# Where expert weights wait for room: four xt tiles, one tile of turned g, and w_out's product in halves

## The chip, the cores and the metric

The kernel runs on one core of a Trainium2 chip. The metric is the device time of one execution in microseconds. Times come from three runs, and the rows from one execution recorded by the hardware profiler. The engines are TensorE (PE; PEld is its weight load), VectorE (DVE), ScalarE (ACT), GpSimd (POOL) and SyncE (SP), which issues every load and store here.

## What is computed

Three parts follow one another. The tokens are 4 x 576 = 2304, and the width is 512.

```python
q, k = rotate(q), rotate(k)                         # 4 x 8 heads x 576 x 64
attn = softmax(q @ k.T / 8, axis=-1); x = attn @ v  # x: 2304 x 512
h = x @ w_in                                        # w_in: 512 x 2048
g = maximum(h, 0) + alpha * minimum(h, 0)
x = g @ w_out                                       # w_out: 2048 x 512
logits = x @ phi                                    # phi: 512 x 32 (8 experts x 4 slots)
d = softmax(logits, axis=0)                         # over the tokens
slot_input = (d.T @ x).reshape(8, 4, 512)
for e in range(8):
    slot_out[e] = maximum(slot_input[e] @ w1[e], 0) @ w2[e]   # 512 x 1024, 1024 x 512
c = softmax(logits, axis=1)                         # over the slots
out = c @ slot_out.reshape(32, 512)
```

The expert weights w1 and w2 are 32 MB in fp32. They are the largest input by far. The weights w_in and w_out come as 8-byte floats.

## The kernel before

**The order of the work.** The kernel is written as operations of a planner (`Plan`, lines 49 to 165). Each operation has an engine, a cost, a due time, the operations that it depends on, and the room that it `takes` or `uses` in a class of buffers. The planner plays them through in time. On each engine it takes, among the operations that are ready and whose room is free, the one with the lowest due time. The order found in this way is fixed in the program, one stream for each engine; SP's stream is all loads and stores in order. A load that must wait for its buffer holds up all that stands behind it on SP.

**Attention and feed-forward.** Attention runs until about 510 us. Its results are `xt` tiles, 8 blocks of 256 tokens, and a ninth block (`blks[8]`, tile `xtail`) of the tails of all four batches. `chunk_events` (line 712) handles a block in 16 chunks f of 128 of the 2048 hidden columns: `ph` = x times w_in (L734, three fp16 products), `rl` on ACT (L742), `g` on DVE (L747). Every second chunk is turned: four transposes `pt` (L753), copied by ACT into a tile `gt` (L758). Two `gt` tiles of 8 KB per partition hold a block, one from f=1, one from f=9. Every fourth chunk adds to the logits `lg` (L764), which are `g` times `wph`, the product of w_out and phi.

w_out itself is never applied to a token. `dispatch_events` (line 777) takes the logits: `lp` (DVE, L802), `lgt` (PE, L806), maximum, exponentials `edt` (ACT, L840), transposes `pd` (L845), `dn` (DVE, L852). Then `pu` (L858) multiplies the weights of the slots by the turned `gt`, and `sacc` (DVE, L867) sums over the blocks. `sacc` (32 slots x 2048) is multiplied by w_out only once, at the end: `pa` (transposes, L1078), `at` (DVE, L1084, four pieces c), `px` (16 matmuls in a loop over g, then c, L1090), which reads eight tiles `wo` of w_out, `xs` (L1095), `pst` (L1100), `phs` (L1107).

**Experts.** `expert_in(j)` for two halves j of w1's output: `ph` (32 matmuls, L1126, steps kc of eight), relu into `xtail`'s space (L1143 ACT, L1145 DVE), transposes `pth` (L1150), and copies that end in `hz` (L1160), a zeroed tile with a slot's values on a diagonal. `expert_out(ch)` for two halves of the output columns: `po` (64 matmuls each, L1180), then `mov` (L1209), the combine `pf` (L1292), `ob` (L1297 DVE, L1299 ACT) and the stores (L1305, L1311). The combine's softmax (`pe`, L1267, `est`, L1271) lies beside the experts.

**Room for weights.** Expert weights `xw` (L1033) are loaded by SP in the order of their use: w1, then w2, in halves of 512 KB (4 KB per partition), or 1 MB where a buffer has room for both halves. `cls_of` (line 1004) says where each goes:

- "x": 26 buffers of 4 KB (`x=2*NB`, NB=13), where attention's buffers were. They also take 16 raw loads of w_out (`late_w`, line 969) and the eight `wo` tiles, so they come round a second time.
- "xt": the four `xt` tiles when their blocks are done. Two take weights; two take the zeroed `hz` (`zero`, line 1064, a memset on POOL).
- "w" and "raw": seven buffers of 8 KB (NW=7): the four quarters of w_in, and three that the `gt` tiles go round in. Loads of class "raw" wait in the plan until the last block's last turn.

The program's addresses say what follows whom. Of the 8 KB buffers, two are held by the last block's `gt` until its `pu` are done. Two of the loads of 1 MB wait for that.

In the trace an fp32 matmul has two records, so eight `pu` show as x16.

## Time and profile before

| | |
|---|---|
| three runs | 671.57 us median (671.46 to 677.29) |
| profiled execution, span from the first to the last instruction | 671.6 us |
| profiled execution, its own time with what lies around the span | 673.49 us |
| busy: PE, DVE, ACT, POOL | 611.0 (91%), 456.0 (68%), 360.5 (54%), 287.8 us (43%) |
| chain that ended last, by engine | PE 71%, DVE 9%, DMA 7%, POOL 6%, ACT 4%, SP's queue 2% |
| mean granted clock of TensorE | 0.963 of 2.4 GHz |
| DMA over the span | 146.57 MB, mean 218 GB/s |

The page gives one execution. A share is an average over stages with different limits; the stage that a change touches is read by itself, in tables of busy time by stretch and in the chain of waits, which follows the work that ended last back from the last instruction. A granted clock of 1.00 is 2.4 GHz and 0.50 is 1.2 GHz; a stretch in between has seen both.

### The profile page before, as it was taken

The numbers are of one execution on the slowest core, as the hardware profiler recorded it, in microseconds if no ns is written. First come the engines' busy times: TensorE is split into PE (matmuls) and PEld (weight loads), VectorE is DVE, ScalarE is ACT, GpSimd is POOL, SyncE is SP. The second block draws the span as 40 slices with busy tenths as digits, with TensorE's granted clock in tenths as the row PEclk, the third lists the DMA queues.
The fourth block names the chain that finished last, engine by engine and source line by source line (L and its number), as shares of the span: only waits on it lengthen the run. The fifth ranks groups of instructions, "written<-read, shape, count | busy, mean of one in ns | idle before, by whom it ended". The sixth has DMA issues, their size and how long they took to land.

```text
span 671.6 us, 13543 instructions
## 1 busy us (share of the span) xinstructions
PE 611.0 (91%) x5072; PEld 433.9 (65%) x5072; DVE 456.0 (68%) x989; ACT 360.5 (54%) x868; POOL 287.8 (43%) x283
## 2 busy tenths in 40 slices
PE   2879968979999999999999999999999999988984
PEld 1545444545888678686767868777776868753452
DVE  4776798787878777877576787677736884334332
ACT  2536545645687686775757676684643434330211
POOL 0698999374647656466353655522320000000000
PEclk9898988978999999999999999999999999999997
DMA  8954274530489796877867784777576984447998
GB/s 294 372 182 136 78 238 135 167 112 15 148 253 271 252 242 191 241 196 214 245 182 216 211 250 134 220 193 205 158 189 252 410 333 150 149 149 301 356 395 295
DMA packets 72672, 146.57 MB, mean 218 GB/s; under 512 B 8352, under 2 KB 37536, under 8 KB 72608
## 3 DMA queue, kind: packets, MB, share of 16 engines
q1 hardware_dynamic: 72608, 145.72, 68.3%
q8 instruction: 40, 0.66, 0.4%
q14 instruction: 24, 0.20, 0.1%
HBM read 108.73 MB, written 29.88 MB: 206 GB/s over the span
## 4 chain that ended last, share of the span: by engine, by line
PE 71%; DVE 9%; DMA 7%; POOL 6%; ACT 4%; SPq 2%; issue 2%; DVEq 0%; ACTq 0%; POOLq 0%
PE ph L734 26%; PE pv L573 13%; PE st L431 7%; PE pt L753 4%; DMA xw<-in_moe_w_dram 4%; PE lg L764 3%; PE pu L858 3%; POOL e L473 3%; PE st L418 3%; PE pt L494 2%; PE pc L537 1%; PE ph L1126 1%; PE rest L267 1%; DMA vt<-in_v_dram 1%; PE st L427 1%
## 5 line engine op out<-in xcount | busy, mean ns | idle before, releaser
L473 POOL TENSOR_SCALAR e<-e,mm 128x576 f32<-128x576 f32 x144 | 122.8, 865 | 152.7 <-DVE mm L449 112.1
L734 PE MATMUL ph<-xt,w 128*128 128x256 f16 x1536 | 184.5, 273 | 1.1 <-DVE g L747 0.4
L734 PEld LDWEIGHTS <-w 128*128 128x128 f16 x1728 | 163.9, 98 | 33.4 <-issue 11.8
L436 DVE TENSOR_REDUCE mm<-st 128x1 f32<-128x576 f32 x144 | 106.2, 742 | 27.6 <-PE st L431 21.4
L441 ACT ACTIVATE e<-st,mm 128x576 f32<-128x576 f32 x144 | 106.3, 739 | 29.4 <-DVE mm L436 26.5
L747 DVE SCALAR_TENSOR_TENSOR g<-rl,oma,ph 128x256 f32<-128x256 f32 x144 | 68.2, 474 | 59.6 <-ACT rl L742 59.0
L321 POOL TENSOR_TENSOR xn<-xn,tabs 128x576 f32<-128x576 f32 x60 | 90.3, 1519 | 30.6 <-DMA xn<-in_q_dram 14.9
L742 ACT ACTIVATE rl<-ph 128x256 f32<-128x256 f32 x144 | 55.0, 382 | 88.0 <-PE ph L734 87.6
L431 PE MATMUL st<-ks,qs 128*128 128x288 f32 x384 | 71.7, 314 | 0.3 <-ACT e L441 0.3
L481 DVE STREAM_TRANSPOSE tb<-e 128x512 f32<-128x512 f32 x96 | 66.6, 700 | 3.7 <-POOL e L473 3.0
L573 PE MATMUL pv<-ET,vt 128*64 128x256 f32 x512 | 63.9, 393 | 2.6 <-DVE qs L346 1.2
L418 PE MATMUL st<-ks 64*128 64x288 f32 (+1 forms) x168 | 46.9, 504 | 16.3 <-DVE ks L329 11.5
L431 PEld LDWEIGHTS st<-ks,qs 128*128 128x128 f32 x384 | 54.7, 191 | 4.7 <-issue 2.4
L758 ACT ACTIVATE gt<-pt 128x512 f32<-128x512 f32 x72 | 43.0, 597 | 15.7 <-PE pt L753 14.2
L573 PEld LDWEIGHTS pv<-ET,vt 128*64 128x64 f32 x512 | 35.6, 139 | 24.3 <-issue 6.1
L418 PEld LDWEIGHTS st<-ks 64*128 64x128 f32 (+1 forms) x168 | 26.7, 216 | 30.2 <-DVE ks L329 11.5
L753 PE MATMUL pt<-idf,g 128*128 128x128 f32 x288 | 43.8, 275 | 0.6 <-DVE g L747 0.4
L753 PEld LDWEIGHTS pt<-idf,g 128*128 128x128 f32 x288 | 33.3, 141 | 4.2 <-issue 1.2
L324 POOL TENSOR_TENSOR xn<-xn 128x576 f32<-128x576 f32 x24 | 35.6, 1482 | 0.9
L494 PE MATMUL pt<-idf,e 128*128 128x128 f32 x192 | 33.0, 306 | 3.3 <-POOL e L473 3.1
L494 PEld LDWEIGHTS pt<-idf,e 128*128 128x128 f32 x192 | 25.1, 159 | 15.1 <-POOL e L473 8.1
L349 ACT ACTIVATE ks<-xn 64x576 fp32r<-64x576 f32 x48 | 32.6, 680 | 0.7
(161 smaller groups left out, 840.2 us busy)
## 6 DMA issues: line engine op xcount, KB each, us to landing
sc<-tb SPq DMA_DIRECT2D x48, 512.0 KB, 4.3
ET<-sc SPq DMA_DIRECT2D x96, 256.0 KB, 5.4
xw<-in_moe_w_dram SPq DMA_DIRECT2D x42, 512.0 KB, 10.1
xn<-in_k_dram SPq DMA_DIRECT2D x16, 576.0 KB, 5.0
xn<-in_q_dram SPq DMA_DIRECT2D x16, 576.0 KB, 4.4
wraw<-in_moe_w_in_dram SPq DMA_DIRECT2D x8, 1024.0 KB, 7.1
wraw<-in_w_out_t_dram SPq DMA_DIRECT2D x8, 1024.0 KB, 5.4
wor<-in_moe_w_out_dram SPq DMA_DIRECT2D x16, 512.0 KB, 10.2
```

Of the source, the lines that this page charges most:

```text
L321: eng.tensor_tensor(e["x"][:, w], e["x"][:, w], tabs[:, (0 if z == "q" else 2) + w], ALU.mult)
L418: nc.tensor.matmul(st[to, j, at:at + w], x, k[rows, z:z + w], start=True, stop=True)
L431: nc.tensor.matmul(st[:, j, 0:288], r["q"][:, 768 * h + 128 * s:768 * h + 128 * s + 128].bitcast(F32R), r["k"][:, a, h, ks].bitcast(F32R), ...
L436: nc.vector.tensor_reduce(c["mm"][:, h:h + 1], c["st", h][:, :, 0:288], axis=AX.XY, op=ALU.max, negate=True)
L441: nc.scalar.activation(c["e"][:, h].rearrange("p (a n) -> p a n", a=2), c["st", h][:, :, 0:288], AF.Exp, bias=c["mm"][:, h:h + 1], accum_o ...
L473: nc.gpsimd.tensor_scalar(c["e"][:, h], c["e"][:, h], c["mm"][:, 6 + h:7 + h], 1.0, ALU.mult, ALU.mult)
L481: nc.vector.transpose(out=c["tb"][:, :, h].rearrange("p (q m) j -> p q m j", q=4), in_=c["e"][:, h, 64 * h:64 * h + 512].rearrange("p (m q ...
L494: nc.tensor.transpose(c["pt", h][:, i], c["e"][:, h, 64 * h + 128 * i:64 * h + 128 * i + 128], idf)
L573: nc.tensor.matmul(pv[r], v[k, 4 * h + i if i < 4 else 8], x, start=(i == 0), stop=(i == 4))
L734: nc.tensor.matmul(ph, wi[j][:, wp, kc, 128 * fo:128 * fo + 128], xt[:, xp, kc, :], start=(n == 0), stop=(n == 3 * KC - 1),)
L747: nc.vector.scalar_tensor_tensor(blk["g", j][:, fo, :], c["r"], oma[:, f:f + 1], c["ph"], ALU.mult, ALU.add)
L753: nc.tensor.transpose(c["pt"][:, t, i, :], blk["g", j][:, fo - 1 + i, 128 * t:128 * t + 128], idf)
```

## The change

1. The x pool gets a 27th buffer of 4 KB per partition.
2. `hz`, both halves, moves from two `xt` tiles into one 8 KB buffer of class "raw". Its memsets wait for the last block's `sacc` (`run["gathered"]`). The four loads of class "xt", which shared two tiles in two rounds, have a tile each. The class "w" takes six loads of 1 MB in place of seven.
3. Raw loads wait in the plan for the last block's turn of f=9 (`turn9`) in place of its last turn.
4. The last block's turns with f above 8, and their copies, get a due time 100 later.
5. `late_w` takes the room of `wo` together with that of its raw load.
6. `at` and `xs` lie in the two halves of `xtail`'s space and need no buffers of their own.
7. `px` is cut into two halves: `turned_a(z)` and `mult_s(z)`, z = 0, 1, with c in the outer loop and g in the inner one. The four `wo` tiles 2g+0 are free after the first half.

```diff
--- before.py
+++ after.py
@@ -208,7 +208,7 @@
 
     plan = Plan(dict(
         xn=3, Q=2, K=2, vt=5, e=3, tb=2, sc=4, ET=2, ec=3, ett=1, tabs=1, st=2, mm=8, pm=3, lg=1, xt=4, w=4, raw=NW - 4,
-        wf=1, rl=2, g=2, wt=1, lp=1, lt=1, edt=1, dn=1, dg=1, x=2 * NB, h1=2, mov=1, tmp=1))
+        wf=1, rl=2, g=2, wt=1, lp=1, lt=1, edt=1, dn=1, dg=1, x=2 * NB + 1, h1=2, mov=1, tmp=1))
     op = plan.op
     PE, ACT, DVE, POOL, DMA = "PE", "ACT", "DVE", "POOL", "DMA"
     FIRST = -10000.0
@@ -779,9 +779,12 @@
         blk["g_op"].append(o)
         if fo % 2:
             s_pt = Slot("pm")
-            o = op(PE, 430, due + 2.5, turn, blk["g_op"][-2:] + [raw_done, blk.get("turn")], takes=[s_pt] + ([s_gt] if f % 8 == 1 else []), uses=[s_pt, s_g, s_gt])
+            late = 100 if blk is blks[8] and f > 8 else 0
+            o = op(PE, 430, due + 2.5 + late, turn, blk["g_op"][-2:] + [raw_done, blk.get("turn")], takes=[s_pt] + ([s_gt] if f % 8 == 1 else []), uses=[s_pt, s_g, s_gt])
             blk["turn"] = o
-            blk["gt_op"].append(op(ACT, 600, d, turned, [o], uses=[s_pt, s_gt]))
+            if f == 9:
+                blk["turn9"] = o
+            blk["gt_op"].append(op(ACT, 600, due + 100 if late else d, turned, [o], uses=[s_pt, s_gt]))
         if fo == 3:
             blk["lg_op"] = op(PE, 430, due + 2.5, logit, blk["g_op"][-4:] + [blk["lg_op"]] + [wph_ops[f - i] for i in range(4)],
                               takes=[] if j else [blk["s_lg"]], uses=[blk["s_lg"], s_g])
@@ -951,7 +954,7 @@
 
     def close_att():
         att_stack.close()
-        xp["p"] = ctx.enter_context(tc.tile_pool(name="xp", bufs=2 * NB))
+        xp["p"] = ctx.enter_context(tc.tile_pool(name="xp", bufs=2 * NB + 1))
         fin["z"] = ctx.enter_context(tc.tile_pool(name="hzp", bufs=1))
         fin["sT"] = phs
         fin["ht"] = wph[:].rearrange("p f s -> p (f s)")[:, 0:256].rearrange("p (k c g i) -> p k c g i", k=4, c=4, g=4)
@@ -990,8 +993,8 @@
                 nc.vector.scalar_tensor_tensor(x, hi, -0x40000000, x, ALU.bitwise_and, ALU.bitwise_or)
 
         d = 990 + 0.1 * f
-        o = order_ops["wo"] = op(DMA, 1456, d, load, [att_done, order_ops.get("wo")], takes=[s_raw], uses=[s_raw])
-        o = op(DVE, 450, d, lambda: conv(0), [o, wo_op.get(j)], takes=[] if z else [s_wo[j]], uses=u)
+        o = order_ops["wo"] = op(DMA, 1456, d, load, [att_done, order_ops.get("wo")], takes=[s_raw] if z else [s_raw, s_wo[j]], uses=u)
+        o = op(DVE, 450, d, lambda: conv(0), [o, wo_op.get(j)], uses=u)
         o = op(DVE, 750, d, lambda: conv(1), [o], uses=u)
         wo_op[j] = op(DVE, 700, d, lambda: conv(2), [o], uses=u)
 
@@ -1002,7 +1005,7 @@
     NT = 2
 
     def cls_of(i):
-        return "xt" if NX <= i < NX + NT else "w" if NX + NT <= i < NX + NT + NW else "x"
+        return "xt" if NX <= i < NX + NT else "w" if NX + NT <= i < NX + NT + NW - 1 else "x"
 
     for base in range(0, len(order), 4):
         for half in range(2):
@@ -1036,7 +1039,7 @@
                 for cut in range(n):
                     due = 1000 + base + 2 * half + 0.2 * (i - base) + (2 * cut if n > 1 else 0)
                     ops.append(op(DMA, 1456 * len(parts) / n, due, lambda cut=cut, load=load: load(cut),
-                                  [att_done, blks[8]["turn"] if slot.cls == "raw" else None] + ops[-1:],
+                                  [att_done, blks[8]["turn9"] if slot.cls == "raw" else None] + ops[-1:],
                                   takes=[] if cut else [slot], uses=[slot]))
                 for part in parts:
                     s_ew[key, part], ew_op[key, part] = slot, ops
@@ -1059,14 +1062,16 @@
 
     fin_open = op(None, 0, 0, open_fin, [o for o in plan.ops if any(s.cls in moe_classes for s in o.uses)])
 
-    hz_zero, s_hz = [], [Slot("xt"), Slot("xt")]
+    hz_zero, s_hz = [], [Slot("raw")] * 2
 
     def zero(j):
-        fin["hz", j] = xtp.tile([128, 8, 4, 4, 8], F32, tag="xt", name="hz")
+        if j == 0:
+            fin["hzs"] = wgt.tile([128, 2, 8, 4, 4, 8], F32, tag="w", name="hz")
+        fin["hz", j] = fin["hzs"][:, j]
         nc.gpsimd.memset(fin["hz", j], 0.0)
 
     for j in range(2):
-        hz_zero.append(op(POOL, 900, 1000, lambda j=j: zero(j), [att_done], takes=[s_hz[j]], uses=[s_hz[j]]))
+        hz_zero.append(op(POOL, 900, 1000, lambda j=j: zero(j), [run["gathered"]] + hz_zero, takes=[] if j else [s_hz[j]], uses=[s_hz[j]]))
     sr = cst.tile([128, 2], F32, name="sr")
     D2 = 2000.0
 
@@ -1077,21 +1082,22 @@
         for c in range(4):
             nc.tensor.transpose(fin["pa"][:, c].rearrange("p g s -> p (g s)"), run["acc"][:, 128 * c:128 * c + 128], idf)
 
-    def turned_a():
-        fin["at"] = fin["p"].tile([128, 4, 4, NS], F32, name="at")
-        for c in range(4):
+    def turned_a(z):
+        if z == 0:
+            fin["at"], fin["xs"] = fin["h1"][:, 1].rearrange("p (c g s) -> p c g s", c=4, g=4), fin["h1"][:, 0]
+        for c in (2 * z, 2 * z + 1):
             iv = inv_w[:].rearrange("p (g h) -> p h g", h=2)[:, c // 2]
             nc.vector.tensor_tensor(fin["at"][:, c], fin["pa"][:, c], iv.unsqueeze(2).to_broadcast([128, 4, NS]), ALU.mult)
 
-    def mult_s():
-        fin["px"] = ps_m.tile([128, DM], F32, tag="pm", name="px")
-        for g in range(4):
-            for c in range(4):
-                nc.tensor.matmul(fin["px"][32 * c:32 * c + 32, :], fin["at"][:, c, g, :], wo[2 * g + c // 2][:, c % 2, :],
-                                 start=(g == 0), stop=(g == 3), tile_position=(0, 32 * c))
+    def mult_s(z):
+        if z == 0:
+            fin["px"] = ps_m.tile([128, DM], F32, tag="pm", name="px")
+        for c in (2 * z, 2 * z + 1):
+            for g in range(4):
+                nc.tensor.matmul(fin["px"][32 * g:32 * g + 32, :], fin["at"][:, c, g, :], wo[2 * g + z][:, c % 2, :],
+                                 start=(c == 0), stop=(c == 3), tile_position=(0, 32 * g))
 
     def kept_s():
-        fin["xs"] = fin["p"].tile([128, DM], F32, name="xs")
         nc.vector.tensor_copy(fin["xs"], fin["px"])
 
     def turn_s():
@@ -1100,8 +1106,12 @@
             nc.tensor.matmul(fin["pst"][:, c], fin["xs"][:, 128 * c:128 * c + 128], sel4[:, 0], start=True, stop=True)
 
     o = op(PE, 430, D2 - 200, turn_a, [run["gathered"]], takes=[s_pa], uses=[s_pa])
-    o = op(DVE, 600, FIRST, turned_a, [o, fin_open], uses=[s_pa])
-    o = op(PE, 3500, D2 - 200, mult_s, [o] + list(wo_op.values()), takes=[s_px], uses=[s_px] + list(s_wo.values()))
+    m = None
+    for z in range(2):
+        o = op(DVE, 440, FIRST, lambda z=z: turned_a(z), [o, fin_open], uses=[s_pa])
+        m = op(PE, 1750, D2 - 200, lambda z=z: mult_s(z), [o, m] + list(wo_op.values()), takes=[] if z else [s_px],
+               uses=[s_px] + [s_wo[2 * g + z] for g in range(4)])
+    o = m
     o = op(DVE, 660, FIRST, kept_s, [o], uses=[s_px])
     o = op(PE, 1100, D2 - 200, turn_s, [o], takes=[s_ps], uses=[s_ps])
     sT_op = op(DVE, 190, FIRST, lambda: nc.vector.tensor_copy(fin["sT"], fin["pst"]), [o, fin_open, *wph_ops.values()], uses=[s_ps])
```

On SP, the end of the stream: `wor` are the raw loads of w_out, `xw` the expert weights. 128x1024 is 512 KB, 128x2x1024 is 1 MB, 128x512 is 256 KB, and what follows are the stores. Before:

```order
136 L978 DMA wor<-in_moe_w_out_dram 128x1024 x16
137 L1033 DMA xw<-in_moe_w_dram 128x1024 x20
138 L1033 DMA xw<-in_moe_w_dram 128x2x1024 x7
139 L1033 DMA xw<-in_moe_w_dram 128x1024 x22
140 L1033 DMA xw<-in_moe_w_dram 128x512 x16
141 L1311 DMA out_dram<-ob 64x2x256 x2
142 L1305 DMA out_dram<-ob 128x4x256 x7
143 L1311 DMA out_dram<-ob 64x2x256 x2
144 L1305 DMA out_dram<-ob 128x4x256
```

and now:

```order
136 L981 DMA wor<-in_moe_w_out_dram 128x1024 x16
137 L1036 DMA xw<-in_moe_w_dram 128x1024 x23
138 L1036 DMA xw<-in_moe_w_dram 128x2x1024 x6
139 L1036 DMA xw<-in_moe_w_dram 128x1024 x21
140 L1036 DMA xw<-in_moe_w_dram 128x512 x16
141 L1321 DMA out_dram<-ob 64x2x256 x2
142 L1315 DMA out_dram<-ob 128x4x256 x8
143 L1321 DMA out_dram<-ob 64x2x256 x2
```

Three more loads of 512 KB stand ahead of the loads of 1 MB, which are six in place of seven, and 21 in place of 22 halves follow. Before, the first of the loads that wait for the last `pu` is the sixth of the seven; now it is the sixth of the six.

On PE, behind the last `ph` of the last block. Before:

```order
4104 L753 MATMUL pt<-idf,g 128x128 x8
4105 L764 MATMUL lg<-g,wph 32x256 x4
4106 L806 MATMUL lgt<-lp,sel_106 128x256
4107 L821 MATMUL ln<-idf,lt 128x32 x2
4108 L845 MATMUL pd<-idf,edt 128x32 x2
4109 L858 MATMUL pu<-gt,dn 32x512 x8
4110 L1078 MATMUL pa<-idf,sacc 128x128 x4
```

and now:

```order
4102 L753 MATMUL pt<-idf,g 128x128 x8
4103 L764 MATMUL lg<-g,wph 32x256 x4
4104 L753 MATMUL pt<-idf,g 128x128 x8
4105 L809 MATMUL lgt<-lp,sel_106 128x256
4106 L824 MATMUL ln<-idf,lt 128x32 x2
4107 L848 MATMUL pd<-idf,edt 128x32 x2
4108 L861 MATMUL pu<-gt,dn 32x512 x8
4109 L1083 MATMUL pa<-idf,sacc 128x128 x4
```

The eight transposes ahead of `lg` were those of f=13 and f=15, while those of f=9 and f=11 stood among the `ph` before. Now f=9 and f=11 stand ahead of `lg`, and f=13 and f=15 behind it, ahead of `lgt`.

On PE, the experts' part. `ph_7430` is the first half of w1's product and `ph_7498` the second. Before:

```order
4113 L1126 MATMUL ph_7430<-xw,phs 32x512 x32
4114 L1126 MATMUL ph_7498<-xw,phs 32x512 x8
4115 L1150 MATMUL pth<-idf,xtail 128x128 x8
4116 L1267 MATMUL pe<-idr,en 128x128 x6
4117 L1180 MATMUL po<-xw,hz 32x256 x16
4118 L1267 MATMUL pe<-idr,en 128x128 x6
4119 L1180 MATMUL po<-xw,hz 32x256 x16
4120 L1267 MATMUL pe<-idr,en 128x128 x6
4121 L1126 MATMUL ph_7498<-xw,phs 32x512 x24
4122 L1150 MATMUL pth<-idf,xtail 128x128 x8
4123 L1180 MATMUL po<-xw,hz 32x256 x48
4124 L1292 MATMUL pf<-mov,est 128x256 x16
```

and now, where they are `ph_7435` and `ph_7503`:

```order
4112 L1136 MATMUL ph_7435<-xw,phs 32x512 x32
4113 L1136 MATMUL ph_7503<-xw,phs 32x512 x8
4114 L1160 MATMUL pth<-idf,xtail 128x128 x8
4115 L1136 MATMUL ph_7503<-xw,phs 32x512 x24
4116 L1277 MATMUL pe<-idr,en 128x128 x6
4117 L1190 MATMUL po<-xw,hz 32x256 x8
4118 L1160 MATMUL pth<-idf,xtail 128x128 x8
4119 L1190 MATMUL po<-xw,hz 32x256 x4
4120 L1277 MATMUL pe<-idr,en 128x128 x6
4121 L1190 MATMUL po<-xw,hz 32x256 x16
4122 L1277 MATMUL pe<-idr,en 128x128 x6
4123 L1190 MATMUL po<-xw,hz 32x256 x52
```

The 24 matmuls that end the second `ph` stood behind three groups of `pe` and 32 `po`; now they follow the first transposes, and all `po` follow them.

## Rows read from the trace of the kernel before

**Rows 1.** Long stretches: engine busy us (instructions), TensorE's granted clock, DMA share, GB/s.

```profile
550.00:600.00 50.00, 49.41 (x459) 38.77 (x457) 20.28 (x46) 19.97 (x45) 0.00 (x0) 1.00 0.44 152
600.00:660.00 60.00, 48.49 (x503) 23.03 (x504) 21.90 (x81) 9.03 (x20) 0.00 (x0) 0.97 0.90 341
```

**Rows 2.** The chain of waits, 594 to 610 us: start, duration, engine, name, line, count.

```profile
594.10 0.44 PE pt L753 x4
...
598.28 0.49 DVE g L747
...
598.82 0.55 PE pt L753 x3
599.36 0.61 PE lg L764 x8
...
600.00 0.87 DVE lp L802 x4
...
603.92 3.36 PE pu L858 x16
...
608.99 0.30 DVE at L1084
```

**Rows 3.** The same chain over 500 to 672 us, an earlier block and the experts' part.

```profile
577.25 1.85 PE pu L858 x16
...
609.34 4.23 PE px L1090 x32
...
615.80 8.79 PE ph L1126 x80
```

**Rows 4.** Short stretches behind the last block, columns as in rows 1.

```profile
603.00:606.00 3.00, 2.38 (x14) 0.78 (x18) 0.30 (x2) 0.24 (x2) 0.00 (x0) 0.72 0.00 0
606.00:609.00 3.00, 1.89 (x12) 0.42 (x4) 1.34 (x6) 0.00 (x0) 0.00 (x0) 0.71 0.15 15
609.00:612.00 3.00, 2.66 (x24) 1.84 (x28) 0.88 (x4) 0.00 (x0) 0.00 (x0) 1.00 1.00 404
609.00:624.00 15.00, 13.50 (x120) 5.72 (x120) 7.63 (x29) 1.27 (x4) 0.00 (x0) 1.00 1.02 410
624.00:627.00 3.00, 2.74 (x34) 1.84 (x30) 1.67 (x12) 1.29 (x3) 0.00 (x0) 1.00 0.56 173
627.00:630.00 3.00, 3.00 (x54) 1.82 (x50) 1.98 (x7) 0.88 (x2) 0.00 (x0) 1.00 1.01 371
```

**Rows 5.** SP's waits, 600 to 615 and 615 to 640: us, times, longest us.

```profile
SPq L1033 <- PE pu L858: 9.0, 1, 9.0
SPq L1033 <- PE px L1090: 3.4, 3, 2.6
...
SPq L1033 <- PE ph L1126: 7.3, 1, 7.3
```

**Rows 6.** The chain of waits, its last `po`.

```profile
657.23 1.06 PE po L1180 x10
```

**Rows 7.** The stretch of the expert products, columns as in rows 1.

```profile
615.80:658.30 42.50, 37.83 (x436) 17.99 (x436) 15.62 (x59) 7.80 (x16) 0.00 (x0) 1.00 1.00 380
```

**Rows 8.** TensorE's waits in that stretch: us, times, longest us.

```profile
PE pth L1150 <- ACT xtail L1143: 1.7, 1, 1.7
PE pf L1292 <- ACT ob L1299: 1.3, 2, 1.0
PE po L1180 <- DVE hz L1160: 0.7, 1, 0.7
PE po L1180 <- DMA xw<-in_moe_w_dram: 0.7, 1, 0.7
```

**Rows 9.** POOL's memsets, and `g` on DVE over 400 to 480 and 530 to 595.

```profile
493.06 0.95 POOL L1066 MEMSET hz<- 128x1024 f32 x1
...
L747 DVE SCALAR_TENSOR_TENSOR g<-rl,oma,ph 128x256 f32<-128x256 f32 x23 | 10.8, 471 | 6.7 <-ACT rl L742 6.7
...
L747 DVE SCALAR_TENSOR_TENSOR g<-rl,oma,ph 128x256 f32<-128x256 f32 x35 | 16.7, 478 | 24.8 <-ACT rl L742 24.7
```

## The prediction

> **What bounds the kernel now.** I read the stretch table first, coarse and then fine, then the chain of waits, then SP's waits, then TensorE's waits. The reader should see three stretches. Until 594 us the feed-forward blocks keep TensorE full: it is busy 49.41 of the 50 us from 550 to 600 at full clock, with DMA at 152 GB/s, so transfers have room there [rows 1]. Nothing on an engine moves in that stretch, only loads do, so the change is worth nothing before 594. From 594 to 608 the last block is dispatched, one dependent step after another: last `g`, transposes, logits `lg`, `lp`, `lgt`, the softmax steps, then `pu`, which begins at 603.92 and ends at 607.28 [rows 2]. From there on the rest of the expert weights must come in. DMA moves 410 GB/s from 609 to 624, and 341 GB/s over 600 to 660 [rows 1, 4]. That last part ends with the last five `po` (ten records) at 657.23 + 1.06 = 658.29 [rows 6]. Write P for the end of the last `pu` (607.28 before). The last `po` then ends at P + 51.0. From there to the end of the span, 13.3 us, are the second half's combine and its stores. The change leaves those alone, and I carry them over as they are.
>
> The sum is made against the profiled execution's span, 671.6 us. The median of the runs is 671.57, so a difference to the span is one to the median.
>
> **Logits ahead of transposes.** Block 8's turns of f=9 and f=11 stood among the last `ph` groups, at 0.44 us each [rows 2]. They now stand behind the last `ph`, in the time in which ACT and DVE make the last `g` (`g` alone is 0.49), so 0.88 comes off ahead of that `g`. The turn of f=15 stood between `g` and `lg` and kept TensorE 0.55 us [rows 2]. It and the turn of f=13 now stand behind `lg`, beside `lp` on DVE, 0.87 us. That cover is 0.87 for about 1.0 of transposes, so `lgt` may lose 0.1, which I leave out. If the cover were gone, 0.55 would come back. The four copies to `gt` on ACT must be there before `pu`. From the end of `lg` (599.97) to `pu` there are 3.95 us, and two late copies need about 1 us behind the last transpose, so they are not late. Gain ahead of `pu`: 0.88 + 0.55 = 1.43. Lower bound: 0.5, if the copies or a PSUM buffer hold `lgt` up. Upper bound: 1.5.
>
> **`pu` and the clock.** The last block's eight `pu` took 3.36 us, and those of an earlier block 1.85 [rows 2, 3]. The granted clock is 0.72 over 603 to 606 and 0.71 over 606 to 609, and 1.00 on both sides [rows 4]. So the low level, 1.2 GHz, was granted for part of that time, after a stretch in which TensorE mostly waited on the softmax steps. Now TensorE is busy for more of that stretch, since two turns lie beside `lp`, and the stretch begins 0.88 earlier. Whether the clock falls again, and on which instruction, no row of before decides. The bounds are a gain of 1.5 (3.36 - 1.85) and a loss of some tenths beyond what the fall costs now. I take the gain, at even chances.
>
> **Weights that come earlier.** SP issues all loads in one order, and its first wait on the last block's `pu`, 9.0 us, blocks everything behind it [rows 5]. Ahead of that wait stood 20 halves of 512 KB and five of 1 MB, which is 15 MiB. Now it is 23 and five, 16.5 MiB: two more `xt` tiles, the 27th `x` tile. Where two 1 MB loads waited for `pu`, one does. Behind `pu` 17.83 MB were left, and now it is 16.25 MB. The 1.57 MB go into 550 to 600, where there is room. At 410 GB/s [rows 4] that is 3.83 us.
>
> The Trainium skill, DMA: Bandwidth & Descriptors, section Specifications, gives about 358 GB/s as what HBM gives one core. By that the same bytes would be worth 4.4 us. The trace disagrees, since 410 GB/s stood for 15 us, and the measurement decides.
>
> **A stall that goes and one that comes.** The last two w1 loads sat in `xt` tiles and waited for the second expert product's first eight `ph`. SP stood 7.3 us for it [rows 5], and DMA ran dry: 173 GB/s over 624 to 627, against 410, is 3 x 237 / 410 = 1.73 us [rows 4]. Now all w1 is there before `pu` and those waits fall on nothing. The next three microseconds at 371 I count as half a recovery, 0.15 each, 0.3 over 627 to 633. What comes: a single 1 MB load (2.56 us at 410) starts behind `pu`. Its data begin some 1.65 us after P, as before (15 GB/s over 606 to 609 is 0.1 us of full rate ahead of 609, then 404) [rows 4], and end at P + 4.2. The next loads wait for the first half of `px`. `px` starts 2.06 us behind P and takes 4.23 now [rows 3]. A half is some 1.9, so SP gets its release at P + 3.95 and data begin at P + 5.6: a gap of 1.4 us that before did not have, since two loads of 1 MB filled it. Bounds for the gap: 0.8 to 2. Load route: last `po` at P + 51.0 - 3.83 - 1.73 - 0.3 + 1.4 = P + 46.5.
>
> **`px` in halves.** Its four column groups each needed another `at`. One `at` takes 0.30 to start with [rows 2], so the groups started apart. Now all four run from the first `at` on. I take 0.6 off 4.23 (bounds 0 and 0.8). `ph` began 8.52 behind P (615.80) [rows 3] and now begins at P + 7.9.
>
> **TensorE as the second bound.** From 615.80 to 658.30 TensorE is busy 37.83 of 42.5 us [rows 7], and every one of those instructions stays. Its waits there are 1.7 on the experts' relu, 1.3 on `ob`, 0.7 on `hz`, 0.7 on a load [rows 8]. The 1.7 goes, since `pe` and `po` now stand between the second `ph` and its transposes. `hz` should be covered in the same way, and the wait on `ob` stays. P + 7.9 + 37.83 + 1.3 = P + 47.0. This is later than the load route's P + 46.5, and it decides by little. Gain behind `pu`: 51.0 - 47.0 = 4.0.
>
> **Sum.** 1.43 + 1.5 + 4.0 = 6.9, so 671.6 - 6.9 = 664.7 us.
>
> **Memsets.** Two of 0.95 us on POOL ran at 493 [rows 9]. They now run right behind the last `pu`, beside `sacc`, `at` and `xs` on DVE. `hz` is wanted only behind the first expert product, some 10 us later, so POOL's own 1.9 us are covered. `g`, a DVE operation with inputs from PSUM and SBUF, took 471 ns with POOL busy and 478 with POOL idle [rows 9], so I cost the memsets at nothing. Upper bound: 1.9 us, if DVE stands while they run.
>
> The Trainium skill, SBUF — State Buffer, section SBUF: two separate sides, has an exclusive lock between VectorE and GpSimd on one port pair, for VectorE operations in a two-port mode or with two SBUF inputs against a GpSimd operation that reads SBUF. By that `at` and `xs`, which read PSUM, would not wait. No row here shows a memset beside them.
>
> **The rivals.**
> - *The clock falls all the same*, on `pu` or on `px`. For it: the softmax chain is as long as before. Against it: the shorter idle time. 664.7 + 1.5 = 666.2. Chance 0.25.
> - *TensorE waits more than I count*: `hz` 0.7 and the estimated 1.7 (relu) do not vanish, or `po` meets the loads closely. 665.5 to 668. For it: the two routes are 0.5 apart, so any wait counts in full. Against it: nine tenths busy already. Chance 0.09.
> - *The memsets hold DVE*: 664.7 + 1.9 = 666.6. Chance 0.03.
> - *The early tiles bring nothing*: loads ahead of `pu` are late themselves, because the 16.5 MiB do not fit into the free time, or SP stands longer on an earlier block's `pu`. Then only the logits count: 671.6 - 1.43 = 670.2. Against it: SP stood 9.0 us on the last `pu`, by its end with nothing in flight (0 GB/s over 603 to 606) [rows 4, 5]. Chance 0.08.
> - *Slower: the low clock lasts through the first expert product.* If TensorE idles longer than now ahead of `ph` and the fall comes there, `ph` (8.79 us) [rows 3] and what follows run at 1.2 GHz. By `pu`'s 3.36 against 1.85, each microsecond at the low level costs 0.45. The gains without the clock are 5.4, so it decides from 12 us at the low level on. Before, the low level held for under 4 us (two rows of 0.72). With all of `ph` and half of `po` at it, 20 us, the time is 666.2 + 9 = 675. Chance 0.05.
>
> **How the numbers follow.** My forecast, clock kept and TensorE just behind the loads, has chance 0.50 and its own range 663.0 to 665.8. Within 1% means 664.85 to 678.3, about what a measurement of this kernel can tell from no change. Of the forecast two thirds (0.33) lie below 664.85, and of the fallen clock a quarter (0.07, if the gap stays at its lower bound and `px` gains more). All other cases lie above. So faster 0.40, slower 0.05, same 0.55. For the range: low 662.8 is the forecast with the waits on `ob` gone and the gap at 0.8. High 667.4 takes in the fallen clock, the memsets and most of the further waits. Outside are "nothing" 0.08, "slower" 0.05, and some 0.06 of the rest.
>
> **What would show it.** In the changed profile: `lg` of block 8 ends 1.4 us earlier, with transposes beside `lp`; `pu` takes 1.85 or 3.4 us, with its granted clock; SP has one load between `pu` and `px`, followed by a gap of some 1.4 us in the DMA rate; no SP wait on the second `ph`, and no stretch at 173 GB/s; TensorE's wait on the relu is gone; the last `po` ends 47.0 us behind the last `pu`, followed by 13.3 us. I am wrong if that last distance stays near 51, if a wait for a weight shows ahead of `pu`, or if DVE's `at` starts late with POOL busy.

## The result, and the profile after

| | before | after |
|---|---|---|
| times of 20 runs each | 674.62 us median (670.58 to 680.13) | 668.11 us median (663.92 to 674.42) |
| profiled execution, span | 671.6 us | 670.3 us |
| second `lg` of the last block begins | 587.7 us | 590.6 us |
| from there to the end of the last `po` (the stretch, below) | 70.6 us | 66.3 us |
| from the last `po` to the end of the span | 13.3 us | 13.4 us |

The ratio is 0.9904 (interval 0.9876 to 0.9933), so the change wins about 1%. The forecast was 664.7 us, or 0.9898 of the 671.57 that the three first runs gave. The ratio came out as forecast. The time did not, and lies 0.7 us above the range: the forecast is a span, to which a run adds 1.9 us, and the kernel before itself is at 674.62 over more runs.

The two profiled spans differ by 1.3 us only. Everything up to the second `lg` is the same work in both programs, yet it came 2.9 us later in the execution of after. The stretch behind it won 4.3 us. The chain of waits of after, start and duration in us:

```profile
590.63 0.57 PE lg L764 x8
...
600.72 0.73 PE lg L764 x8
601.45 1.02 PE pt L753 x8
...
605.46 1.99 PE pu L861 x16
607.54 1.95 DVE idr L1232
...
610.59 5.34 PE px L1097 x32
...
655.85 1.06 PE po L1190 x10
```

Against [rows 2, 3, 6]: from the second `lg` to the end of the last `lg` 10.8 us (12.2 before), `pu` at full clock in 1.99 (3.36), then two that are worse: the cast to `idr`, a step of 0.23 before, takes 1.95, and `px` takes 5.34 (4.23). The chain of before had these lines there:

```profile
607.36 0.23 DVE idr L1222
607.59 0.67 DVE sacc L867
608.26 0.04 issue
608.30 0.67 PE pa L1078 x4
```

The stretches behind the last block in the profile of after, columns as in rows 1:

```profile
603.00:606.00 3.00, 1.28 (x13) 0.63 (x16) 1.26 (x5) 0.91 (x4) 0.00 (x0) 1.00 0.38 154
606.00:609.00 3.00, 1.39 (x16) 0.18 (x8) 1.46 (x3) 0.00 (x0) 1.43 (x2) 1.00 0.26 22
609.00:612.00 3.00, 2.07 (x12) 0.81 (x16) 1.69 (x9) 0.00 (x0) 0.41 (x1) 0.73 0.84 336
612.00:615.00 3.00, 3.00 (x24) 0.76 (x20) 0.00 (x0) 0.00 (x0) 0.00 (x0) 0.70 0.00 0
615.00:618.00 3.00, 1.87 (x16) 0.97 (x8) 0.88 (x2) 0.00 (x0) 0.00 (x0) 1.00 0.98 329
```

The low clock lies within 609 to 615 now, on `px` instead of `pu` [rows 4]. And DMA moves nothing for the three microseconds from 612: the gap that the forecast put at 1.4 us. SP's waits, 600 to 615, and TensorE's, 618 to 657 (us, times, longest):

```profile
SPq L1036 <- PE pu L861: 7.2, 1, 7.2
SPq L1036 <- PE px L1097: 6.0, 1, 6.0
...
PE pf L1302 <- ACT ob L1309: 1.3, 2, 1.0
PE pth L1160 <- ACT est L1281: 0.4, 1, 0.4
```

SP stood 6.0 us on `px` (3.4 before, in three waits [rows 5]). Of its 7.3 us on the experts' `ph` 1.9 are left, in two waits from 615 to 640. The stretch at 173 GB/s is gone, and so are TensorE's waits of 1.7 on the relu and 0.7 on `hz` [rows 8].

### The profile page after: what moved, and what is told of

The parts are those of the page before. It is cut to its first block, busy times and chain, and to the rows that moved or that the text cites. A ratio compares the mean times of both kernels' runs of the same rounds, so it can differ in the third digit from the quotient of the medians.

```text
span 670.3 us, 13561 instructions
## 1 busy us (share of the span) xinstructions
PE 610.9 (91%) x5072; PEld 432.3 (64%) x5072; DVE 457.7 (68%) x989; ACT 360.1 (54%) x868; POOL 287.2 (43%) x283
## 4 chain that ended last, share of the span: by engine, by line
PE 71%; DVE 9%; DMA 7%; POOL 5%; ACT 3%; SPq 2%; issue 2%; DVEq 0%; ACTq 0%; POOLq 0%
PE ph L734 24%; PE pv L573 12%; PE st L431 6%; PE st L418 4%; PE pt L753 4%; DMA ET<-sc 4%; PE pt L494 3%; PE pu L861 3%; PE lg L764 2%; POOL e L473 2%; PE ph L1136 2%; PE po L1190 2%; PE rest L267 2%; PE pc L537 1%; DVE mm L436 1%
## 5 line engine op out<-in xcount | busy, mean ns | idle before, releaser
L1071 POOL MEMSET hz<- 128x1024 f32 x2 | 1.8, 952 | 111.6 <-PE pu L861 111.6
```

## Experiments

The change has 20 timed runs, each other kernel 6 to 12, each set beside runs of the kernel before. The sets lie on at least three chips, so what is compared are the ratios to the kernel before. "Stretch" is the time from the second `lg` to the end of the last `po` in the profiled execution, of which each kernel has one.

| run | ratio (interval) | stretch | low clock in the stretch |
|---|---|---|---|
| before, the first profile | | 70.6 | `pu` |
| before again | 1.001 (0.998 to 1.004) | 73.4 | `pu` to `px`, 10.2 us |
| late turns only | 0.9956 (0.9925 to 0.9987) | 70.0 | `ph` |
| changed, early turns | 0.9917 (0.989 to 0.9945) | 69.5 | `pu` to `px`, 10.2 us, and `ph` |
| changed, 26 x buffers | 0.9937 (0.991 to 0.9964) | 64.7 | none |
| changed | 0.9904 (0.9876 to 0.9933) | 66.3 | `px` |
| changed, first repeat | 0.9846 (0.9812 to 0.988) | 64.0 | none |
| changed, second repeat | 0.9873 (0.9835 to 0.991) | 65.1 | none |
| changed, cast late | 0.9871 (0.9827 to 0.9916) | 66.6 | `pu` |
| changed, `px` whole | 0.988 (0.9847 to 0.9914) | 65.1 | none |
| cast late, transposes in the waits | 0.9866 (0.9824 to 0.9908) | 64.2 | none |
| the same again | 0.9874 (0.9826 to 0.9922) | 63.8 | none |
| the same, `px` whole | 0.9863 (0.9826 to 0.99) | 62.6 | none |
| cast late, `px` whole | 0.9856 (0.9814 to 0.9899) | 64.2 | `pu` |

**The cast late.**

```diff
-    idr_op = op(DVE, 135, D2 + 2, round_id, [fin_open])
+    idr_op = op(DVE, 135, D2 + 2, round_id, [fin_open, sT_op])
```

> The changed kernel with one dependency more: the cast to idr waits for phs, so it leaves its place ahead of sacc on DVE and comes after phs, when the memsets of hz are over. In the changed kernel this cast took 1.95 us beside the memsets instead of 0.23 and sacc followed it; pa began 2.1 us after the end of the last pu, px 3.1 us. Theory A, the memset holds the cast alone and not sacc or at: pa begins 0.8 us after pu, px about 1.9, with the memsets beside them, and the stretch from the second lg of the last block to the end of the last po is at least 1.2 us under the changed kernel's 66.3. Theory B, a memset holds whatever DVE runs beside it: sacc takes 1.9 us in the cast's place, pa begins at 2.1 as before this edit, and nothing is won. The clock: if the shorter wait ahead of px keeps it at full speed, px takes 3.6 in place of 5.3 and the stretch loses up to 1.7 us more; if not, px stays above 4.

In the changed kernel, DVE and POOL side by side (start, duration, idle before in brackets):

```profile
607.54 1.95 DVE L1232 CAST idr<-idf 128x128 fp32r<-128x128 f32 x1 [2.13 <-PE pu L861]
607.68 1.81 DVE L870 SCALAR_TENSOR_TENSOR sacc<-sacc,sts,pu 128x512 f32<-128x512 f32 x1
...
607.57 1.84 POOL L1071 MEMSET hz<- 128x1024 f32 x2 [111.56 <-PE pu L861]
```

and with the cast late:

```profile
604.84 0.75 DVE L870 SCALAR_TENSOR_TENSOR sacc<-sacc,sts,pu 128x512 f32<-128x512 f32 x1 [3.52 <-PE pu L861]
...
604.86 1.84 POOL L1071 MEMSET hz<- 128x1024 f32 x2 [112.91 <-PE pu L861]
...
601.37 3.29 PE L861 MATMUL pu<-gt,dn 128*32 128x512 f32 x16 [0.32 <-DVE dn L855]
605.64 0.66 PE L1083 MATMUL pa<-idf,sacc 128*128 128x128 f32 x4 [0.98 <-DVE sacc L870]
```

`sacc` takes its 0.75 us right beside a memset, and `pa` begins 0.98 us behind `pu` in place of 2.16: theory A. A memset holds the cast of one SBUF tile into another, and neither `sacc` nor `at`. Nor does it hold the three small operations of DVE between SBUF tiles that follow (128x1, on `ssum` and `sr`): they ran beside the memsets in 0.21, 0.15 and 0.17 us, as in the kernel before. So it is not SBUF alone that makes an operation wait. The rest of the chain came earlier as expected, yet the stretch was not shorter, since here the clock fell on `pu` (3.29), and the second load that `px` freed landed 3.6 us behind the first.

**The memsets late, which became a repeat.**

```diff
+    plan.also(hz_zero[0], [sT_op])
```

> The changed kernel with the memsets of hz waiting for phs, so that POOL is idle beside sacc, at and xs. Theories A and B both expect the cast to idr at 0.23 us and pa 1.0 us after the end of the last pu, px 2.06 us after it as in the kernel before; the stretch from the second lg to the end of the last po 1.1 us under 66.3, and up to 1.7 more where the clock does not fall on px. What could be lost: the memsets now lie beside the combine's first DVE operations, which have 8.8 us of ph as cover, so nothing on the path is expected. Against the run with the cast late it is 0.2 us slower by theory A (the cast is back ahead of sacc), and at least 0.9 us faster by theory B.

The dependency is one of the planner's. It fixes the order on POOL, where the memsets stand alone, so the program's streams stayed those of the changed kernel, and the memsets started at the same place. The run counts as a repeat. It shows how much one program differs by itself:

```profile
599.80 1.92 PE L861 MATMUL pu<-gt,dn 128*32 128x512 f32 x16 [0.32 <-DVE dn L855]
603.00 0.66 PE L1083 MATMUL pa<-idf,sacc 128*128 128x128 f32 x4 [1.27 <-DVE ssum L876]
604.03 3.64 PE L1097 MATMUL px<-wo,xtail 128*32 128x512 f32 x32 [0.38 <-DVE xtail L1090]
...
601.87 1.06 DVE L1233 CAST idr<-idf 128x128 fp32r<-128x128 f32 x1 [2.13 <-PE pu L861]
```

The cast waits for one memset (1.06) and not for two (1.95), and no low clock falls into the stretch: `px` takes 3.64. The chain's end says what bounds it, a wait for loads and then the last ten records of `po`:

```profile
642.55 5.31 DMA xw<-in_moe_w_dram
...
647.90 1.06 PE po L1191 x10
```

**The changed kernel again.** No edit.

> The changed kernel once more, beside the others on one chip. Theory A (its executions differ by the low clock, at the start of attention and behind the last block): from the second lg to the last po 64.1 us where the clock holds and up to 66.7 where it falls; the second lg begins between 583.8 and 591.6, the later the longer the clock was low before it; ratio to the kernel before 0.985 to 0.990. Rival: the stretch is what differs by chip, not by clock, and shows 66.3 with the clock at full speed.

The clock held, the cast took 1.06, and the stretch was 65.1, where theory A had 64.1 for a held clock: 1.1 us more than the first repeat's, with TensorE's instructions alike up to `ph`. The last load landed 47.2 us behind `pu`, and 46.1 there. In both traces a load lands 1.28 us behind the one before it when the stream is full, and once or twice in a stream one needs 2 to 2.7. That alone makes about a microsecond from one execution to the next; what causes it stays open.

**Early turns.**

```diff
-            late = 100 if blk is blks[8] and f > 8 else 0
+            late = 0
```

> The changed kernel without the late due times: the last block's turns of f=9 to 15 come as soon as they can. Theory A (the logits' lead is worth its transposes): from the second lg of the last block to the start of pu 1.35 us more than the changed kernel's 14.8, so 16.2; the loads behind pu move with it, and the last po comes 1.4 us later, time plus 0.2%. Rival: the end hangs on bytes alone and the last po does not move; time plus 0.

The second `lg` to `pu` took 16.2 us, as theory A said. The time is 0.9917, against 0.9904, 0.9846 and 0.9873 of the changed kernel: slower by some 0.1 to 0.7%, where 0.2 was expected. Its interval is clear only of the first repeat's, which was timed beside it (670.8 and 665.6 us). In its profile the low clock lasts longer, and its ten timed runs have a mean granted clock of 0.960 over the span, the six of the first repeat 0.966:

```profile
603.00:606.00 3.00, 1.83 (x12) 0.10 (x4) 1.04 (x3) 0.00 (x0) 1.01 (x2) 0.50 0.12 10
606.00:609.00 3.00, 2.53 (x12) 1.11 (x16) 1.23 (x9) 0.00 (x0) 0.91 (x1) 0.50 0.91 325
609.00:612.00 3.00, 3.00 (x20) 0.74 (x16) 0.00 (x0) 0.00 (x0) 0.00 (x0) 0.50 0.07 23
```

**Late turns only**, on the kernel before.

```diff
+            late = 100 if blk is blks[8] and f > 8 else 0
-            o = op(PE, 430, due + 2.5, turn, ...
+            o = op(PE, 430, due + 2.5 + late, turn, ...
-            blk["gt_op"].append(op(ACT, 600, d, turned, ...
+            blk["gt_op"].append(op(ACT, 600, due + 100 if late else d, turned, ...
```

> The kernel before with the late turns alone; tiles, hz and px as before. Theory A: from the second lg to the start of pu 1.35 us less than before's 16.2, and the last po 1.4 us earlier, as two 1 MB loads wait for pu and move with it; 0.2% off the time of the kernel before, so the other 0.75% of the change come from the loads. Rival: the 27th buffer and the xt tiles give nothing, and this kernel has the change's whole 1%.

`pu` came 14.8 us behind the second `lg` (16.2 before), and the time is 0.9956: the late turns bring 0.1 to 0.8%, more than the 0.2 of theory A in the middle. The low clock has a part in that: the mean granted clock is 0.962 over its 12 timed runs and 0.957 over the 21 of the kernel before beside them, an estimated 7 us less at the low level (the share of time at 1.2 GHz is twice what the mean lacks to 1.00). What the change wins beyond this run comes from its other edits together. The profile's stretch, 70.0, lies only 0.5 under before's, since the low clock fell on the first `ph` here, 10.49 us for 8.79.

**`px` whole.** `turned_a` and `mult_s` as in the kernel before, `at` and `xs` in `xtail`'s space.

> The changed kernel with px as it was before: g outside, c inside, four column groups that each wait for their own at. Theory A, by the loads' issue times in the traces: halves free their first wo tile 1.94 us behind the start of px and four at once, the old form frees its first 1.28 us behind it and the others one after the other. So here the first load that px frees is issued some 0.6 us earlier and px takes 4.2 in place of 3.6 us; the loads end 0.3 to 0.6 earlier or the same, and the kernel is within 0.1% of the changed one. Rival, as the prediction had it: halves win 0.6 us on TensorE and lose nothing, so this run is 0.6 us slower.

Loads freed by `px` were issued 1.28 us behind its start (1.94 with halves), and `px` took 4.21. The 0.1% between theory A and the rival is less than the intervals can tell. The stretch at full clock, 65.1, is that of the second repeat and 1.1 above the first's, so no gain of the halves shows. The last load landed 47.3 us behind `pu`, no earlier than with halves: the first loads that `px` freed landed 1.9 and 1.6 us behind one another, and a later one 2.4.

**26 x buffers.**

```diff
-        ... x=2 * NB + 1, h1=2, mov=1, tmp=1))
+        ... x=2 * NB, h1=2, mov=1, tmp=1))
-        xp["p"] = ctx.enter_context(tc.tile_pool(name="xp", bufs=2 * NB + 1))
+        xp["p"] = ctx.enter_context(tc.tile_pool(name="xp", bufs=2 * NB))
```

> The changed kernel with the x pool back at 26 buffers: one load of 512 KB fewer ahead of the last pu. Theory A (the end hangs on the bytes left behind pu): at 410 GB/s 1.28 us more from the end of the last pu to the last load and to the last po, at the same clock; 0.2% slower. Rival (TensorE is the bound there): no change in the last po, the last load comes closer to it.

0.9937 is slower than each of the three sets of the changed kernel, by 0.3 to 0.9%, though its interval meets that of the first. So the buffer most likely counts, and by these numbers for more than the 0.2% of theory A. The profile shows neither: the last load came 46.9 us behind `pu`, against 46.1 and 47.2 in the repeats, and the stretch is 64.7. Where the time lies stays open.

**The kernel before again.** No edit.

> The kernel before, unchanged, timed and profiled like the others. It tells what a difference of nothing looks like and whether the profile of before was a usual one. Theory A (what differs between executions is attention's part and the place where the clock falls): the ratio holds 1.000 in its interval, the second lg begins up to 3 us from 587.7, the stretch from there to the last po is 69 to 71 us, with another instruction at the low clock or none. Rival: the profile of before was typical, with the clock falling on pu at the same place.

The ratio is 1.001, as expected. The profile is of the slowest of its 12 runs (680.45 us) and lies outside what theory A allowed: the second `lg` begins 4.0 us later than in the first profile, and the stretch is 73.4. The low clock lay over `pu`, `pa` and part of `px`:

```profile
606.00:609.00 3.00, 1.75 (x12) 0.88 (x16) 0.82 (x4) 0.75 (x3) 0.00 (x0) 0.67 0.00 0
609.00:612.00 3.00, 2.58 (x15) 0.20 (x4) 0.27 (x2) 0.00 (x0) 0.00 (x0) 0.50 0.00 0
612.00:615.00 3.00, 1.95 (x8) 1.44 (x12) 1.94 (x8) 0.00 (x0) 0.00 (x0) 0.50 0.61 231
```

**Transposes in TensorE's waits**, with the cast late. `filler(n)` is called inside the functions of `lgt`, `ln`, `pd`, `pu` (last block), `pa`, `px` and `pst`.

```diff
+    def filler(n):
+        for i in range(n):
+            nc.tensor.transpose(fl["t"][:, i % 2, :], idf, idf)
```

> The kernel with the cast late, and 27 transposes of the identity into an unused PSUM tile laid into TensorE's waits from lgt to the first expert product (6 behind lgt, 3, 2, 6 behind pu, 2, 6 behind px, 2); nothing reads them. A transpose takes 0.11 us, so each group is shorter than the wait that it lies in. Theory A (the granted clock falls because TensorE waits here): the clock stays at full speed from lgt to the last po, pu takes 1.92, px 3.64, and the stretch from the second lg to the last po is 63.4 to 64.4 us in the profile, where single executions of the variants with the same loads have shown 64.1 to 66.7; the times of the rounds lie closer together than those of the run with the cast late (663.3 to 671.5) and their median some 1 us lower. Rival: the clock falls all the same, by something other than these waits: pu 3.3 or px over 5 in the profile, and the same spread. Second rival: the transposes hold the chain up, 0.1 to 0.5 us slower.

> The kernel with the cast late and the transposes in TensorE's waits, once more. If the transposes keep the clock (theory A), this second profile shows no low clock between the second lg and the last po either, pu at 1.92 and px at 3.64, and the stretch 63.4 to 64.4. If the first profile was luck, it shows a fall on pu, px or ph in about half of the cases, as the kernels without them do. Median at or under that of the changed kernel beside it, by 0 to 1.5 us.

The second profile, where the groups fit into the waits:

```profile
605.77 0.88 PE L796 MATMUL fl<-idf 128*128 128x128 f32 x6
606.80 0.66 PE L1098 MATMUL pa<-idf,sacc 128*128 128x128 f32 x4 [0.16 <-DVE sacc L885]
607.29 0.38 PE L796 MATMUL fl<-idf 128*128 128x128 f32 x2
607.84 3.64 PE L1113 MATMUL px<-wo,xtail 128*32 128x512 f32 x32 [0.17 <-DVE xtail L1106]
```

No low clock in the stretch in three profiles of three (the third is the next run). Of seven profiles with late turns and the new tiles but no such transposes, four have none either. The medians (664.9 and 666.4) are those of the repeats (665.6 and 666.4). The mean granted clock of the timed runs is 0.964 to 0.968 with the transposes, and 0.963 to 0.967 in the seven sets of the changed kernel and its variants without them. So it is not shown that the transposes do it, nor that they bring time.

**Cast late and `px` whole**, with and without the transposes.

> The cast late, the transposes in TensorE's waits, and px in its old form (g outside): what the runs so far would put together. From the traces: with px whole its first wo tile is free 1.28 us behind the start of px in place of 1.94, so the first load that px frees is issued at 3.3 us behind the last pu (3.9 with halves), and px takes 4.2 in place of 3.6. Theory A, the end hangs on the loads: the last load lands 0 to 0.6 us earlier than with halves (46.35 behind pu), about the same time. Rival, TensorE's 0.6 us decide: 0.6 us later. Clock as with the transposes: pu at 1.92, no fall before the last po.

> The changed kernel with px in its old form and the cast late, without the transposes in the waits. With the transposes this showed 62.65 us from the second lg to the last po, the last load 44.6 us behind the last pu, and four loads freed by px one after the other from 3.3 us on. Theory A (the loads are the bound, and the old px frees its tiles in the order in which SP wants them): the same 62.5 to 63.2 us if the clock holds, the last load 44.6 to 45.2 behind pu where no load takes over 2 us from its forerunner, and 1.2 us less than the same kernel with halves (63.8 and 64.3). Rival (that profile was luck, or the transposes did it): 63.8 or more at full clock. Where the clock falls, the stretch says nothing between the two; the issue times of the loads behind px still do. Time of the rounds: 0.983 to 0.988 of the kernel before.

In both the last load landed 44.6 us behind `pu`, earlier than in any of the changed kernels with halves (45.9 to 48.4). With the transposes the stretch was 62.6, the shortest of all. Without them it was 64.2 with the low clock on `pu` (3.49 for 1.92, so an estimated 62.6 without it). Both fit theory A; the run with `px` whole and the cast early (47.3) had the early issue times but not the early landing. Where the time lies, the rows of DMA behind `pu` show, at nearly the same P (602.9 and 602.6). The changed kernel, second repeat:

```profile
603.00:606.00 3.00, 1.44 (x12) 0.70 (x16) 2.27 (x9) 0.00 (x0) 1.92 (x2) 1.00 0.65 177
606.00:609.00 3.00, 2.86 (x28) 0.65 (x20) 0.00 (x0) 0.00 (x0) 0.00 (x0) 1.00 0.67 257
609.00:612.00 3.00, 1.86 (x16) 1.25 (x20) 1.82 (x6) 0.02 (x1) 0.00 (x0) 1.00 0.85 276
```

and with the cast late and `px` whole:

```profile
603.00:606.00 3.00, 2.03 (x16) 1.39 (x20) 1.86 (x8) 0.00 (x0) 1.64 (x2) 1.00 0.67 227
606.00:609.00 3.00, 2.84 (x26) 1.27 (x18) 0.12 (x1) 0.00 (x0) 0.00 (x0) 1.00 0.97 329
609.00:612.00 3.00, 1.99 (x20) 1.29 (x24) 1.83 (x7) 0.02 (x1) 0.00 (x0) 1.00 1.01 396
```

(227 + 329 + 396 - 177 - 257 - 276) x 3 us is 726 KB, or 1.8 us at 410 GB/s. Some 0.3 of it are the earlier P, and 0.3 the late cast, by which `px` starts 2.0 us behind `pu` in place of 2.3. The old `px` frees its tiles g by g, by the issue times in the order in which SP wants them: four loads go out one after the other from 3.3 us behind `pu`. The halves let two out at 3.9 and the next ones at 5.8. In its timed runs this version (0.9856) is under the changed kernel's 0.9904, but the intervals overlap, and it does not differ from the repeats. It beats the kernel before clearly; over the changed kernel only the profiles put it ahead.

## Why the prediction was right or wrong

**The level: wrong, and this alone put the time outside the range.** The step that failed is the sentence that a difference to the span is one to the median: it takes the span of 671.6 for a run of 671.57. That the two numbers are alike is chance. The profiled execution itself took 673.49, and in every timed run here the time is some 1.9 us more than the span. So a span of 664.7 is a run of 666.6, and the range 662.8 to 667.4 is one of 664.7 to 669.3, which holds 668.11. The three runs were low, too: they showed 671.46, 671.57 and 677.29, a spread of 6 us, and I built the range from the costs of the edits alone. In six sets of 11 to 23 runs the kernel before stands at 674.1 to 676.1. With its measured ratio the change would be at 665.1 on the old level.

**What moves the level.** Up to the second `lg` every kernel here issues the same instructions but for the place of some loads and of POOL's two memsets, but that `lg` begins between 583.9 and 591.7 us. The mean granted clock of the first 160 us goes with it. Four of the 14 profiles, before, before again, after, first repeat, with `lg` at 587.7, 591.7, 590.6 and 585.0:

```profile
0.00:160.00 160.00, 126.12 (x663) 73.55 (x663) 119.60 (x215) 78.67 (x182) 115.45 (x101) 0.88 0.54 180
```

```profile
0.00:160.00 160.00, 125.34 (x641) 72.17 (x641) 118.45 (x210) 77.26 (x179) 114.62 (x100) 0.86 0.54 180
```

```profile
0.00:160.00 160.00, 125.36 (x643) 72.17 (x643) 118.46 (x210) 77.26 (x179) 114.63 (x100) 0.86 0.54 180
```

```profile
0.00:160.00 160.00, 125.98 (x689) 74.58 (x690) 124.96 (x219) 80.91 (x186) 117.65 (x102) 0.90 0.54 180
```

Over all 14: at 0.90 585.0; at 0.89 583.9 to 588.4; at 0.88 585.6 to 589.0; at 0.87 589.1 and 589.5; at 0.86 590.6 and 591.7. In the 20 timed runs of the change, too, those from 670 us on have 0.956 to 0.963 over the span and those under 667 us 0.964 to 0.969. That the clock is the cause was not tried by an edit.

**The difference: right in size** (forecast 0.9898; measured 0.9904, repeats 0.9846 and 0.9873). The stretch was forecast at 63.7 (70.6 - 6.9) and was 66.3, 64.0 and 65.1. That the sum fits is in part luck: of its steps some cost more than forecast, and the low clock, which the prediction priced from the one profile of before, weighs more in the usual runs. Their mean granted clock is 0.958 over 78 runs of the kernel before and 0.964 over 32 of the changed one, an estimated 9 us less at the low level. Where in the span these lie the runs do not say; at the prediction's 0.45 for each, and all on the chain, they would by estimate be up to 4 of the 6.5 us. By its steps:

- *Logits*: 1.43 forecast; 1.4 at the end of `lg`, 1.35 at the start of `pu`. Right.
- *The clock*: `pu` kept it in the profile of after, so 1.4 came, but the low clock fell on `px` and took 1.6 (5.34 for 3.76 in the repeats). The rival had named `px`. Of the three profiles of this program two are without it.
- *Memsets*: costed at nothing, chance 0.03; they cost 1.1 us in the profile (`pa` 2.1 us behind `pu`, 1.0 before) and 0.2 in the repeats. The step named `sacc`, `at` and `xs` as what runs beside them and left out the cast to `idr`, which stands ahead of `sacc` on DVE. The rule of the Trainium skill that I weighed there (SBUF — State Buffer, section SBUF: two separate sides) fits what the runs show in this: `sacc`, which reads PSUM, did not wait, the SBUF-to-SBUF cast did, for whole memsets. I applied it to the wrong instructions. That rule of the Trainium skill gives the ports to whichever operation starts first; by the records the cast starts 0.03 us ahead of the memset and still waits. That the cast runs in a two-port mode, as the rule would have it, no run shows.
- *The gap behind `pu`*: 1.4 forecast. In the profile DMA stood for 3 us, with the late and slow `px`; at full clock, second repeat, 177, 257 and 276 GB/s over 603 to 612 against 410 from P + 1.65 are 2.2 us lost. With the cast late and `px` whole the same sum of the rows above (227, 329 and 396) gives 0.7. So the gap is mis-sized, above its bound of 2, and the step behind it is "`px` in halves": I compared the halves with the old form on TensorE only (0.6, which came: 3.64 for 4.21) and not by the order in which they free tiles.
- *Bytes and the stall on `ph`*: the stretch at 173 GB/s is gone, as forecast. The 3.83 us for the bytes cannot be read apart; the run with 26 buffers supports the direction.
- *TensorE as the second bound*: mis-sized. In all three profiles of this program the last `po` ended 1.1 us behind the last load, and in the two repeats the chain ends in waits for loads, so there the loads decided. In the profile of after, where `ph` began 10.7 us behind `pu` in place of 7.9, TensorE had no such wait and both ended together. The 37.83 us were too much: in the runs with the cast late and `px` whole the same 436 records are busy 35.7 us. The stall on the relu went, as forecast. From `pu` to the last `po`: 47.0 forecast, 47.2, 48.3 and 49.5 measured.
- *The tail*: 13.3 carried over, 13.4 measured. Right.

Of the rivals, the low clock on `px` and the held DVE both came in the profiled execution. The slower rival's mechanism, a low clock that lasts, showed for 10.2 us in the run with early turns and in before again, not in one with late turns. The clocks of the timed runs bear that out: the late turns added to the kernel before moved the mean from 0.957 to 0.962, and taken from the changed kernel from 0.964 to 0.960. So the late turns shorten the low clock. By what, no run shows: TensorE does the same transposes either way, and with more of them in its waits no change of the clock shows.

## What to carry to other kernels

A forecast of a time needs the spread of the level as much as the difference: three runs that differ by 6 us are no base for a range of 5, and the span of a profile is not the time of a run. When work moves to a new place, list every instruction that is queued there on the other engines, the small ones too; the one that was left out was the one that waited. A buffer's release has an order, and a form that is faster on its engine can free buffers in an order that the queue behind does not want.

## What the runs showed of the hardware

- A memset of 0.95 us on POOL holds a cast from SBUF to SBUF on DVE (128x128) for whole memsets (1.06 or 1.95 us for 0.23), while a DVE operation that reads PSUM runs beside it at 0.75 us, and three of 128x1 between SBUF tiles at 0.15 to 0.21.
- The same program has stretches at 1.2 GHz at other places from one execution to the next: behind the last block 3.4 or 10.2 us in the kernel before, none or 3.4 in the changed one, and in the first 160 us of the changed one a mean clock of 0.86 to 0.90.
- In a full stream of 512 KB loads, each landing 1.28 us behind the last, single ones need 2 to 3.2 us.
- Four of the last block's eight groups of transposes, put behind its last `ph`, raised the mean granted clock of the kernel before from 0.957 (21 runs) to 0.962 (12 runs).
